# Decayed linear attention and two FFNs on one core: scores in tiles of 64 by 64, quarter-megabyte loads, one update moved ahead

## The chip, the core and the metric

The kernel runs on one core of a Trainium2 chip. Its engines work side by side: PE (TensorE) does the matmuls, DVE (VectorE), ACT (ScalarE) and POOL (GpSimd) work on tiles in the on-chip memory, and SP (SyncE) issues the DMAs, which 16 DMA engines carry out. Each engine runs its own instructions in order and waits on semaphores for the others. The metric is the device time of one execution in microseconds, lower is better, as a median over several runs.

## The reference

Per batch and head (2 by 8, sequence 768, head size 64), attention goes through blocks of 64 tokens and carries a 64 by 64 state:

```
intra = (q_b k_b^T * Dmask) v_b            Dmask[i,j] = lam^(i-j) for i >= j, else 0
inter = (q_b * lam^(pos+1)) state
out_b = intra + inter
state = lam^64 * state + (k_b * lam^(63-pos))^T v_b
```

The result, as 1536 tokens by 512, goes through two feed-forward layers with 2048 hidden units: h = x w_in; g = h * tanh(softplus(h)) in the first, g = h * relu6(h + 3) / 6 in the second; then g w_out.

## The kernel before, in words

Attention works on chunks of 128 tokens, two of the reference's blocks, all eight heads of a batch at once: 12 chunks, of which chunks 0 to 5 are one batch and 6 to 11 the other. A chunk's input `att[c]` is one row of 8 KB for each of 128 partitions, 1 MB: keys and queries with the head size down the partitions (columns 0 to 1023, two heads on the two halves of the partitions), then keys and values with the tokens down the partitions (columns 1024 to 2047). `load_raw(c, i)` loads half i of it, 512 KB.

What is done for a chunk, with the lines of the kernel before:

- `scores(c)` (line 194, PE): for each of 4 head pairs and each of its 2 heads, one matmul of a 64 by 128 weight tile (the keys) on 128 columns (the queries), into one of two PSUM banks by head. A float32 matmul leaves two records in the trace, so a chunk has 16.
- `weigh(c)` (line 216, DVE): the scores times the table of decays.
- `scale_k(c)` (line 206): the token-major keys times their decay, in place. For chunks 0 and 1 on DVE, else on POOL. `scale_q(c)` (line 210, POOL): the queries times theirs, once the scores have read them.
- `update(c)` (line 234, PE): scaled keys times values, weight tiles of 128 by 64, for the state that the next chunk needs.
- `attend(c)`: weighed scores times values (line 242, PE, weight tiles of 128 by 64), then state times scaled queries (line 248, PE, weight tiles of 64 by 64) unless the chunk starts a batch.
- `tokens(c)` splits the result into a high and a low part for the FFN (line 101 ACT, line 105 DVE), and `carry` inside it makes the next state (line 259 DVE; its fade on ACT or POOL).

The order on each engine is written out by hand: `hold` keeps program order on PE, DVE, ACT and POOL. After `warm_up(12)`, the tables, `scores(0)`, `warm_up(4)`, `scale_k(0)` and `weigh(0)`, the loop over c issues `update(c)`, for c = 0 also `scores(1)`, `weigh(1)` and `scale_k(1)` on DVE, then `attend(c)`, `scores(c + 2)`, `scale_q(c + 1)`, `tokens(c)`, `scale_k(c + 2)`, `weigh(c + 2)`. At chunks 8 to 10 the conversion of the first weight units is woven in (line 332 ACT, line 337 DVE).

All loads go through SP's queue in the order written (`follow`): the decay table, chunks 0 to 7, then after each of chunks 0 to 3 a chunk from 8 to 11, with the first two weight units (`load_w`, line 309, 512 KB each) between the halves of chunks 10 and 11, and three more weight units after them. The scheduler gives DMAs eight semaphores in turn, so that a DMA is issued once the one eight places before it has landed.

After the attention come the two FFNs, in 128-column tiles of the hidden units (lines 371 and 380, then 752 and 769), with weights converted from their packed form on the way.

Of the kernel before, what the change touches and what calls it, by code (L numbers as in the profile page):

```python
# [11 lines left out]
U16 = mybir.dt.uint16  # L12
# [10 lines left out]
def decay_attention__mish_ffn__hswish_ffn_kernel(  # L23
# [8 lines left out]
    nc = tc.nc  # L32
    NCH = att.shape[0]
# [8 lines left out]
    def hold(engine, ins):  # L42
        if engine in held:
            tc.keep_in_program_order(ins)
        return ins
# [38 lines left out]
    def two_banks(kind):  # L84
        i = bank_turn[kind]
        assert i % 2 == 0
        bank_turn[kind] = (i + 2) % len(BANKS[kind])
        return BANK[:, BANKS[kind][i]:BANKS[kind][i] + 2]
# [41 lines left out]
    def follow(ins):  # L130
        if loads:
            tc.add_manual_dep(
                ins.ins, loads[-1].ins.name,
                mybir.DependencyInfo(mybir.DependencyClass.NoSync, mybir.DependencyReason.DATA), reason="order of loads",
            )
        loads.append(ins)
    raw_t = {}
# [3 lines left out]
    def load_raw(c, i):  # L141
        if c >= NCH:
            return
        if i == 0:
            j = c % 8 - 4
            if j >= 0:
                raw_t[c] = early[:, 2048 * j:2048 * j + 2048]
            else:
                pool = lent_p if c % 4 > 1 else raw_p
                raw_t[c] = pool.tile([128, 2048], F32, tag="raw", name="raw")  # L150
        s = slice(i * 1024, (i + 1) * 1024)
        follow(nc.sync.dma_start(out=raw_t[c][:, s], in_=att[c, :, s]))  # L152

    def qk(c):
        t = raw_t[c]
        return (t[:, i:i + 512].rearrange("p (a i) -> p a i", a=4) for i in (512, 0))

    def kv(c):
        t = raw_t[c]
        return t[:, 1024:1536], t[:, 1536:2048]  # L160

    def reverse():
        rr = mask.rearrange("j h p i -> j p h i")[:, :, :, 127:128]
        return rr.to_broadcast([128, 4, 2, 64])

    def decay_tables():
# [9 lines left out]
        def powers(o, i, first, drive):  # L176
            tc.keep_in_program_order(nc.vector.tensor_tensor_scan(
                out=o, data0=small[:, i:i + 1].to_broadcast([128, 128]), data1=drive, initial=first,
                op0=ALU.mult, op1=ALU.add,
            ))  # L180
# [4 lines left out]
        for p in range(4):  # L185
            powers(lampow[:, p], p, 1.0, zero)

    def scores(c, kind):
        qT, kT = qk(c)
        sc = two_banks(kind).rearrange("p h (a i) -> p h a i", a=4)  # L190
        for p in range(4):
            for h2 in range(2):
                r = slice(h2 * 64, h2 * 64 + 64)
                hold("tensor", nc.tensor.matmul(sc[:, h2, p, :], lhsT=kT[r, p, :], rhs=qT[r, p, :], start=True, stop=True))  # L194
        sc_t[c] = sc

    def carries(c):
        return c % CPB < CPB - 1

    def follows(c):  # L200
        return c % CPB > 0

    def scale_k(c, name="gpsimd"):
        if carries(c):
            kk = kv(c)[0].rearrange("j (p h d) -> j p h d", p=4, h=2)
            hold(name, getattr(nc, name).tensor_tensor(out=kk, in0=kk, in1=reverse(), op=ALU.mult))

    def scale_q(c, name="gpsimd"):
        qT, kT = qk(c)
        hold(name, getattr(nc, name).tensor_tensor(out=qT, in0=qT, in1=lampow, op=ALU.mult))  # L210
# [3 lines left out]
    def weigh(c):  # L214
        out = masked[c] = amat[c % 2]
        hold("vector", nc.vector.tensor_tensor(out=out, in0=sc_t.pop(c), in1=mask, op=ALU.mult))  # L216

    half = [slice(0, 64), slice(64, 128)]

    def heads():  # L220
        for a in range(2):
# [5 lines left out]
    def update(c, kind):  # L227
        kn, vn = kv(c)
        uo = two_banks(kind)
        u = uo[:, 0, 256:512].rearrange("p (a d) -> p a d", a=4)  # L230
        uo_t[c] = u, uo[:, :, 0:256].rearrange("p b (a i) -> p b a i", a=2)
        if carries(c):
            for a, e, p, h2, s in heads():
                hold("tensor", nc.tensor.matmul(u[half[h2], p], lhsT=kn[:, s], rhs=vn[:, s], start=True, stop=True))  # L234

    def attend(c):
        qT, kT = qk(c)
        kn, vn = kv(c)
        o = [uo_t[c][1][:, i] for i in range(2)]
        last = not follows(c)  # L240
        for a, e, p, h2, s in sorted(heads(), key=lambda x: x[3]):
            hold("tensor", nc.tensor.matmul(  # L242
                o[h2][half[e], a], lhsT=vn[:, s], rhs=masked[c][:, h2, p, :],
                start=(a == 0), stop=(last and a == 1), skip_group_check=True,
            ))
        if follows(c):
            for a, e, p, h2, s in heads():
                hold("tensor", nc.tensor.matmul(  # L248
                    o[h2][half[e], a], lhsT=state[c % 2][half[h2], p, :], rhs=qT[half[h2], p, :],
                    start=False, stop=(a == 1), skip_group_check=True,  # L250
                ))
        del raw_t[c]
# [19 lines left out]
    def tokens(c):  # L272
        o = uo_t[c][1]
        off = (c % 4) * 128
        hi, lo = (X[c // 4][:, i, :, off:off + 128].rearrange("p (b a) i -> p b a i", b=2) for i in range(2))
        split_hi(hi, o)
        carry(c)
        split_lo(lo, hi, o)
# [2 lines left out]

    unit_turn = [0]
    SHARED = [(0, 1), (3, 0), (5, 0), (3, 1)]
    shared = {}
    busy = set()
    slots = {}

    def load_w(w, t, half, count):
        if w is w1 and count == 2:
            st = stage_p.tile([128, 2, 512], U64, tag="st2", name="st")  # L290
        elif w is w1 and (t, half) in SHARED:
            i, j = divmod(SHARED.index((t, half)), 2)
            if j == 0:
                shared[i] = stage_p.tile([128, 2, 512], U64, tag="st2", name="st")
            st = shared[i][:, j:j + 1]
        elif w is w1:
            i = unit_turn[0] % 3
            unit_turn[0] += 1
            slots[w is w1, t, half] = {i}
            st = ring[:, i:i + 1]  # L300
        else:
            i = unit[t // 2, half] % 2
            slots[w is w1, t, half] = {0, 1} if i == 0 else {3}
            st = ring[:, 0:2] if i == 0 else spare[0][:, 16:24].bitcast(U64).rearrange("p (t i) n -> p t (i n)", t=2)
        taken = slots.get((w is w1, t, half), set())
        assert not taken & busy
        busy.update(taken)
        words = w[t:t + count, half].rearrange("t p n -> p t n").bitcast(U16)
        ins = nc.sync.dma_start(out=st.bitcast(U16)[:, :, 0:2047], in_=words[:, :, 1:2048])
        if w is w1:  # L310
            follow(ins)
        stage_t[w is w1, t, half] = st

    def staged(w, t, half):
# [193 lines left out]
    def start_next(between=None):  # L508
        begin(*plan[begun[0]], between=between)
        begun[0] += 1  # L510
# [82 lines left out]
    warm_up(12)  # L593
    decay_tables()
    scores(0, "y")
    warm_up(4)
    scale_k(0, "vector")
    weigh(0)
    for c in range(NCH):
        update(c, "y" if c == NCH - 1 else "a" if c % 2 == 0 else "h")  # L600
        if c == 0:
            scores(1, "y")
            weigh(1)
            scale_k(1, "vector")
        attend(c)
        if c < NCH - 2:
            scores(c + 2, "y")
        if c < NCH - 1 and follows(c + 1):
            scale_q(c + 1)
        if c == 10:  # L610
            start_next(lambda: tokens(10))
        else:
            tokens(c)
        if c < NCH - 2:
            scale_k(c + 2)
        if c == 8:
            start_next(lambda: weigh(10))
        elif c < NCH - 2:
            weigh(c + 2)
        if c == 9:  # L620
            finish_next()
        if c < 4:
            load_raw(c + 8, 0)
            if c > 1:
                load_w(*plan[c - 2])
            load_raw(c + 8, 1)
        if c == 3:
            for i in (2, 3, 4):
                load_w(*plan[i])
# [12 lines left out]
    for n in range(STEPS):  # L642
# [23 lines left out]
        layer, k, t = seq[n][:3]  # L666
# [200 lines left out]
    for j in range(R):  # L867
        k, p = runs[j]
# [3 lines left out]
        for f, (name, ms) in enumerate(FILLS):  # L872
# [3 lines left out]
            c = COPY[name]  # L876
            hold("scalar", nc.scalar.activation(out=c, in_=bank_[:, 0:n], func=ACTF.Copy))  # L877
            c = c.rearrange("p (i n) -> p i n", n=256)
            if f == 1:
                hold("vector", nc.vector.tensor_tensor(  # L880
                    out=F[:, 2:4], in0=COPY["a"].unsqueeze(1).to_broadcast([128, 2, 256]), in1=c, op=ALU.add
                ))
            elif f == 2:
                hold("vector", nc.vector.tensor_tensor(
                    out=F[:, 0:4:3], in0=F[:, 3:4].to_broadcast([128, 2, 256]), in1=c, op=ALU.add
# [97 lines left out]
```

## Time and profile before

| | us |
|---|---|
| median of 3 runs (555.13 to 555.54) | 555.5 |
| the profiled execution's own time | 554.98 |
| its span | 553.2 |
| PE busy | 546.4 (99%) |
| DVE busy | 393.9 (71%) |
| ACT busy | 313.6 (57%) |
| POOL busy | 22.9 (4%) |

The span runs from the first to the last instruction that the profiler saw; the execution's own time has 1.8 us around it. A busy time is the sum of an engine's instructions, so 99% says that PE nearly always has something in it, not that it works at its peak. Weight loads (PEld) run beside the matmuls and are listed apart. In the rows "<-" in brackets is what ended the idle time ahead of an instruction.

### The profile page before, as it was taken

The numbers are of one execution on the slowest core, as the hardware profiler recorded it, in microseconds if no ns is written. First come the engines' busy times: TensorE is split into PE (matmuls) and PEld (weight loads), VectorE is DVE, ScalarE is ACT, GpSimd is POOL, SyncE is SP. The second block draws the span as 40 slices with busy tenths as digits, with TensorE's granted clock in tenths as the row PEclk, the third lists the DMA queues.
The fourth block names the chain that finished last, engine by engine and source line by source line (L and its number), as shares of the span: only waits on it lengthen the run. The fifth ranks groups of instructions, "written<-read, shape, count | busy, mean of one in ns | idle before, by whom it ended". The sixth has DMA issues, their size and how long they took to land.

```text
span 553.2 us, 9679 instructions
## 1 busy us (share of the span) xinstructions
PE 546.4 (99%) x3888; PEld 491.3 (89%) x3888; DVE 393.9 (71%) x613; ACT 313.6 (57%) x488; POOL 22.9 (4%) x24
## 2 busy tenths in 40 slices
PE   8999999999999999999999999999999999999997
PEld 4887888888888888888888999999999999999996
DVE  6668876551136757796772798887898887987776
ACT  2457898873255756867482555555455555454551
POOL 1761000000000000000000000000000000000000
PEclk9999999999999999999999999999999999999999
DMA  8995556450045998889979969994698975688912
GB/s 295 412 394 200 170 200 211 144 186 6 0 153 208 359 356 285 325 302 420 377 282 403 426 270 379 345 367 154 227 322 319 355 307 190 229 319 356 386 64 76
DMA packets 25356, 149.04 MB, mean 269 GB/s; under 512 B 2400, under 2 KB 5600, under 8 KB 18400
## 3 DMA queue, kind: packets, MB, share of 16 engines
q1 hardware_dynamic: 25312, 148.44, 70.6%
q8 instruction: 30, 0.49, 0.4%
q14 instruction: 14, 0.11, 0.1%
HBM read 115.92 MB, written 32.51 MB: 268 GB/s over the span
## 4 chain that ended last, share of the span: by engine, by line
PE 95%; DMA 2%; DVE 1%; ACT 1%; SPq 0%; issue 0%; DVEq 0%; ACTq 0%
PE bank L371 24%; PE bank L380 24%; PE bank L752 22%; PE bank L769 21%; PE bank L194 2%; DMA raw<-att 2%; PE bank L242 2%; PE bank L248 1%; PE bank L234 1%; SPq L152 0%; DVE FS L789 0%; DVE up L105 0%; DVE early L216 0%; ACT up L101 0%; DVE work L780 0%
## 5 line engine op out<-in xcount | busy, mean ns | idle before, releaser
L105 DVE TENSOR_TENSOR g<-x,g 128x512 fp32r<-128x512 f32 x48 | 33.0, 689 | 56.0 <-ACT g L401 52.4
L380 PE MATMUL bank<-g,up 128*128 128x512 f32 x288 | 70.3, 390 | 0.0
L371 PE MATMUL bank<-X,up 128*128 128x512 f32 x288 | 69.2, 389 | 0.0
L400 ACT ACTIVATE x<-bank 128x512 f32<-128x512 f32 x48 | 28.5, 593 | 70.7 <-PE bank L371 70.7
L371 PEld LDWEIGHTS bank<-X,up 128*128 128x128 f32 x288 | 54.1, 188 | 11.2
L380 PEld LDWEIGHTS bank<-g,up 128*128 128x128 f32 x288 | 53.6, 188 | 10.6
L877 ACT ACTIVATE two<-bank 128x512 f32<-128x512 f32 x48 | 28.7, 597 | 55.7 <-PE bank L752 55.7
L877 ACT ACTIVATE work<-bank 128x256 f32<-128x256 f32 (+1 forms) x48 | 23.6, 491 | 59.2 <-PE bank L752 59.2
L752 PE MATMUL bank<-X,up 128*128 128x256 f32 x384 | 54.6, 283 | 0.0
L752 PEld LDWEIGHTS bank<-X,up 128*128 128x128 f32 x384 | 49.9, 192 | 0.2 <-ACT work L877 0.2
L380 PE MATMUL bank<-g,lowA 128*128 128x512 f32 x180 | 43.2, 389 | 0.0
L371 PE MATMUL bank<-X,lowA 128*128 128x512 f32 x180 | 43.2, 389 | 0.0
L769 PE MATMUL bank<-up,lowB 128*128 128x256 f32 x318 | 43.1, 283 | 0.0
L780 DVE SCALAR_TENSOR_TENSOR work<-x,work 128x512 f32<-128x512 f32 x48 | 33.0, 688 | 14.0 <-ACT x L779 13.9
L769 PEld LDWEIGHTS bank<-up,lowB 128*128 128x128 f32 x318 | 40.3, 192 | 0.0
L371 PEld LDWEIGHTS bank<-X,lowA 128*128 128x128 f32 x180 | 33.8, 188 | 7.0
L380 PEld LDWEIGHTS bank<-g,lowA 128*128 128x128 f32 x180 | 33.8, 188 | 7.0
L107 DVE SCALAR_TENSOR_TENSOR lowA<-spare,lowA 128x1792 fp32r<-128x1792 f32 x16 | 32.4, 2022 | 10.3 <-ACT lowA L101 10.3
L752 PE MATMUL bank<-X,lowA 128*128 128x256 f32 x270 | 38.2, 283 | 0.0
L769 PE MATMUL bank<-up,up 128*128 128x256 f32 x276 | 37.7, 283 | 0.0
L752 PEld LDWEIGHTS bank<-X,lowA 128*128 128x128 f32 x270 | 35.2, 192 | 0.3
L769 PEld LDWEIGHTS bank<-up,up 128*128 128x128 f32 x276 | 35.1, 192 | 0.0
(122 smaller groups left out, 979.8 us busy)
## 6 DMA issues: line engine op xcount, KB each, us to landing
up<-wc SPq DMA_DIRECT2D x19, 1792.0 KB, 10.1
wc<-lowA SPq DMA_DIRECT2D x16, 1792.0 KB, 10.0
lowA<-wc SPq DMA_DIRECT2D x13, 1792.0 KB, 8.6
ring<-w SPq DMA_DIRECT2D x24, 511.8 KB, 3.5
raw<-att SPq DMA_DIRECT2D x16, 512.0 KB, 10.2
ring<-w SPq DMA_DIRECT2D x8, 1023.5 KB, 7.7
spare<-w SPq DMA_DIRECT2D x8, 1023.5 KB, 8.3
lowB<-wc SPq DMA_DIRECT2D x6, 1280.0 KB, 7.3
```

What stands on the lines that cost most here:

```text
L105: hold("vector", nc.vector.tensor_tensor(out=lo, in0=src, in1=f32(hi), op=ALU.subtract))
L107: hold("vector", nc.vector.scalar_tensor_tensor(out=lo, in0=src, scalar=scale, in1=f32(hi), op0=ALU.mult, op1=ALU.subtract))
L194: hold("tensor", nc.tensor.matmul(sc[:, h2, p, :], lhsT=kT[r, p, :], rhs=qT[r, p, :], start=True, stop=True))
L234: hold("tensor", nc.tensor.matmul(u[half[h2], p], lhsT=kn[:, s], rhs=vn[:, s], start=True, stop=True))
L242: hold("tensor", nc.tensor.matmul(o[h2][half[e], a], lhsT=vn[:, s], rhs=masked[c][:, h2, p, :], start=(a == 0), stop=(last and a == 1), sk ...
L371: hold("tensor", nc.tensor.matmul(h, lhsT=W[t][:, a, kt * 128:kt * 128 + 128], rhs=X[k][:, b, kt, :], start=(kt, a, b) == order[0], stop=( ...
L380: hold("tensor", nc.tensor.matmul(y[e], lhsT=l, rhs=r, start=(first and i == 0), stop=(last and i == 2),))
L400: hold("scalar", nc.scalar.activation(out=x, in_=h, func=ACTF.Mish))
L752: hold("tensor", nc.tensor.matmul(bank_[:, 256 * i:256 * i + 256], lhsT=w[:, a, kt * 128:kt * 128 + 128], rhs=x[:, b, kt], start=(i == 0 a ...
L769: hold("tensor", nc.tensor.matmul(acc[:, i], lhsT=GB[j % 2][:, gi, a, i * 128:i * 128 + 128], rhs=w[:, b], start=(first and i == 0 and q = ...
L780: hold("vector", nc.vector.scalar_tensor_tensor(out=F, in0=x, scalar=6.0, in1=F, op0=ALU.min, op1=ALU.mult))
L877: hold("scalar", nc.scalar.activation(out=c, in_=bank_[:, 0:n], func=ACTF.Copy))
```

## The change

Scores become 16 matmuls of 64 by 64 weight tiles in place of 8 of 64 by 128: the keys' 128 tokens are taken in two halves, which go to the two halves of the PSUM partitions. A raw half is loaded by two DMAs of 256 KB, and so are five weight units of the first layer; the number of DMAs in flight gets no rule of its own. Chunk 2's scores and weighing move from chunk 0's turn to chunk 1's, behind `update(1)`; chunk 1's `scale_k` moves from DVE to POOL.

```diff
--- before.py
+++ after.py
@@ -148,8 +148,9 @@
             else:
                 pool = lent_p if c % 4 > 1 else raw_p
                 raw_t[c] = pool.tile([128, 2048], F32, tag="raw", name="raw")
-        s = slice(i * 1024, (i + 1) * 1024)
-        follow(nc.sync.dma_start(out=raw_t[c][:, s], in_=att[c, :, s]))
+        for j in (2 * i, 2 * i + 1):
+            s = slice(j * 512, (j + 1) * 512)
+            follow(nc.sync.dma_start(out=raw_t[c][:, s], in_=att[c, :, s]))
 
     def qk(c):
         t = raw_t[c]
@@ -185,13 +186,16 @@
         for p in range(4):
             powers(lampow[:, p], p, 1.0, zero)
 
+    half = [slice(0, 64), slice(64, 128)]
+
     def scores(c, kind):
         qT, kT = qk(c)
         sc = two_banks(kind).rearrange("p h (a i) -> p h a i", a=4)
         for p in range(4):
-            for h2 in range(2):
-                r = slice(h2 * 64, h2 * 64 + 64)
-                hold("tensor", nc.tensor.matmul(sc[:, h2, p, :], lhsT=kT[r, p, :], rhs=qT[r, p, :], start=True, stop=True))
+            for m in half:
+                for h2 in range(2):
+                    r = half[h2]
+                    hold("tensor", nc.tensor.matmul(sc[m, h2, p, :], lhsT=kT[r, p, m], rhs=qT[r, p, :], start=True, stop=True))
         sc_t[c] = sc
 
     def carries(c):
@@ -214,8 +218,6 @@
     def weigh(c):
         out = masked[c] = amat[c % 2]
         hold("vector", nc.vector.tensor_tensor(out=out, in0=sc_t.pop(c), in1=mask, op=ALU.mult))
-
-    half = [slice(0, 64), slice(64, 128)]
 
     def heads():
         for a in range(2):
@@ -281,6 +283,7 @@
 
     unit_turn = [0]
     SHARED = [(0, 1), (3, 0), (5, 0), (3, 1)]
+    FIRST_UNITS = [(0, 0), (1, 0), (2, 0), (0, 1), (3, 0)]
     shared = {}
     busy = set()
     slots = {}
@@ -306,9 +309,11 @@
         assert not taken & busy
         busy.update(taken)
         words = w[t:t + count, half].rearrange("t p n -> p t n").bitcast(U16)
-        ins = nc.sync.dma_start(out=st.bitcast(U16)[:, :, 0:2047], in_=words[:, :, 1:2048])
-        if w is w1:
-            follow(ins)
+        ends = (0, 1024, 2047) if w is w1 and (t, half) in FIRST_UNITS else (0, 2047)
+        for a, b in zip(ends, ends[1:]):
+            ins = nc.sync.dma_start(out=st.bitcast(U16)[:, :, a:b], in_=words[:, :, a + 1:b + 1])
+            if w is w1:
+                follow(ins)
         stage_t[w is w1, t, half] = st
 
     def staged(w, t, half):
@@ -601,9 +606,12 @@
         if c == 0:
             scores(1, "y")
             weigh(1)
-            scale_k(1, "vector")
+            scale_k(1)
+        elif c == 1:
+            scores(2, "y")
+            weigh(2)
         attend(c)
-        if c < NCH - 2:
+        if 0 < c < NCH - 2:
             scores(c + 2, "y")
         if c < NCH - 1 and follows(c + 1):
             scale_q(c + 1)
@@ -615,7 +623,7 @@
             scale_k(c + 2)
         if c == 8:
             start_next(lambda: weigh(10))
-        elif c < NCH - 2:
+        elif 0 < c < NCH - 2:
             weigh(c + 2)
         if c == 9:
             finish_next()
```

## Rows read from the trace of the kernel before

**Rows 1.** the page, part 4: the chain that ended last, share by engine.

```profile
PE 95%; DMA 2%; DVE 1%; ACT 1%; SPq 0%; issue 0%; DVEq 0%; ACTq 0%
```

**Rows 2.** stretches: us, each engine's busy time (instructions), clock, DMA share, GB/s.

```profile
45.28:537.00 491.72, 491.72 (x3075) 446.61 (x3072) 351.57 (x545) 292.05 (x441) 0.00 (x0) 1.00 0.71 270
```

**Rows 3.** chain of waits, first 46 us: start us, us, what.

```profile
3.15 9.24 DMA raw<-att
12.44 1.16 PE bank L194 x16
```

**Rows 4.** PE's weight loads in time, 17.9 to 21.5 us: start, us, line, shapes.

```profile
18.20 0.43 PEld L248 LDWEIGHTS bank<-raw,state 64*64 64x64 f32 x16 [0.17 <-issue]
18.79 0.97 PEld L194 LDWEIGHTS bank<-early 64*128 64x128 f32 x16 [0.17 <-issue]
19.89 0.55 PEld L234 LDWEIGHTS bank<-raw 128*64 128x64 f32 x16
20.35 0.86 PEld L242 LDWEIGHTS bank<-early,raw 128*64 128x64 f32 x16
21.38 0.21 PEld L248 LDWEIGHTS bank<-raw,state 64*64 64x64 f32 x8 [0.17 <-POOL early L210]
```

**Rows 5.** the same, 8.3 to 10.2 us.

```profile
8.38 0.55 PEld L234 LDWEIGHTS bank<-raw 128*64 128x64 f32 x16 [0.42 <-DVE raw L206]
8.99 0.97 PEld L194 LDWEIGHTS bank<-raw 64*128 64x128 f32 x16
```

**Rows 6.** the same, 12.3 to 16.8 us.

```profile
13.53 0.55 PEld L234 LDWEIGHTS bank<-raw 128*64 128x64 f32 x16
13.99 0.86 PEld L242 LDWEIGHTS bank<-early,raw 128*64 128x64 f32 x16
```

**Rows 7.** POOL in time, 8 to 28 us: start, us, line, operation.

```profile
10.25 1.27 POOL L210 TENSOR_TENSOR raw<-raw,lampow 128x512 f32<-128x512 f32 x1 [9.81 <-PE bank L194]
13.77 1.06 POOL L206 TENSOR_TENSOR raw<-raw,mask 128x512 f32<-128x512 f32 x1 [2.25 <-DMA raw<-att]
```

**Rows 8.** SP's issue of chunk 11's first half; its KB and us to landing.

```profile
26.52 0.33 SPq L152 DMA_DIRECT2D raw<-att  x1
...
raw<-att SPq DMA_DIRECT2D x1, 512.0 KB, 10.5
```

**Rows 9.** landing of the decay table; issue to landing over line 152.

```profile
small<-lam SPq DMA_DIRECT2D x1, 70.0 KB, 2.1
...
DMA to landing us min/median/max: 4.9/10.2/11.4
```

**Rows 10.** DMA of 15:25, 340:344, 503:505.2 and 1.5:2.25 us; last number: share of 16 engines.

```profile
DMA packets 1120, 4.10 MB, mean 410 GB/s; under 512 B 124, under 2 KB 124, under 8 KB 1118
q1 hardware_dynamic: 1118, 4.07, 101.3%
...
DMA packets 140, 1.65 MB, mean 412 GB/s; under 512 B 15, under 2 KB 15, under 8 KB 15
q1 hardware_dynamic: 140, 1.65, 98.8%
...
DMA packets 338, 0.95 MB, mean 434 GB/s; under 512 B 48, under 2 KB 48, under 8 KB 304
q1 hardware_dynamic: 338, 0.95, 108.2%
...
DMA packets 121, 0.06 MB, mean 84 GB/s; under 512 B 9, under 2 KB 121, under 8 KB 121
q1 hardware_dynamic: 121, 0.06, 37.9%
```

**Rows 11.** PE's weight loads in time, 36 to 45.5 us.

```profile
40.05 0.97 PEld L194 LDWEIGHTS bank<-raw 64*128 64x128 f32 x16 [0.17 <-issue]
43.51 0.85 PEld L242 LDWEIGHTS bank<-early,raw 128*64 128x64 f32 x16 [0.44 <-DVE early L216]
```

**Rows 12.** ACT in time, 35 to 46 us.

```profile
37.51 0.65 ACT L332 ACTIVATE tops<-ring 128x512 f16<-128x512 bf16 x1
```

## The prediction, made before the changed kernel was run

> **What bounds the kernel now.** I read the page first: the chain that ended last is 95% TensorE [rows 1]. Then the stages: from 45.28 to 537 us PE is busy for 491.72 of 491.72 us, without a gap [rows 2]. All edits lie before that stretch (the first weight units feed it), so whatever brings its first matmul forward brings the end forward by as much, provided the weights keep up. The question is only: when does the stretch that begins at 45.28 us begin?
>
> For that I read the chain of waits of the first 46 us. It runs through the first loads until 12.39 us, when the first half of chunk 2 lands, and its scores start at 12.44 us [rows 3]; from there it is PE nearly throughout. So the attention has two limits in turn: landing until 12.4 us, then PE. I then took PE's weight loads in order of time, because their starts show when one group of matmuls gives way to the next. A middle chunk reads 18.20 (line 248, state times query), 18.79 (line 194, scores), 19.89 (line 234, updates), 20.35 (line 242), 21.38 (line 248 again): 3.18 us [rows 4].
>
> **Part 1: scores in 64 by 64 tiles.** Line 194 loads 64 by 128 tiles and takes 19.89 − 18.79 = 1.10 us for 16 records (8 float32 matmuls, two records each). The new form is 16 matmuls, 32 records, of the very form of line 248: a 64 by 64 weight tile, 128 columns moved, alternating over both row halves and both column halves. Line 248 takes 18.79 − 18.20 = 0.59 us for 16 records. What of that is the change of tile shape behind it? Line 234 takes 0.46 us where line 242, of its own weight shape, follows [rows 4], and 8.99 − 8.38 = 0.61 us where line 194 follows [rows 5]: a change costs 0.15 us. So line 248's form costs 0.44 us per 16 records, plus 0.15 us where the shape changes next. New scores: 2 × 0.44 + 0.15 = 1.03 us, only 0.07 us less than 1.10. The larger gain is at the neighbour: where scores follow line 248 directly, the change between them goes. Before: 0.59 + 1.10 = 1.69 us; after: 3 × 0.44 + 0.15 = 1.47 us; 0.22 us saved. Scores 3 to 7 and 9 to 11 follow a line 248: 8 × 0.22 = 1.76 us. Scores 8 follow line 242 (chunk 6 starts a sequence) and scores 2 will stand between lines 234 and 242: 2 × 0.07 = 0.14 us. Scores 0 and 1 lie before the landing that binds and count nothing. Bounds: no gain (1.10 us and both changes kept) to 1.90 us; a loss, 32 records at line 194's own 69 ns, is excluded by line 248's 37 ns. I take the full sum, since line 248 is the same form with operands of the same shape.
>
> **Part 2: chunk 1's update ahead of chunk 2's scores.** Before, PE idles until 12.44 us for chunk 2, then runs scores 2 to 13.53, update 1 to 13.99, and attend 1 [rows 6]. After, the 0.46 us of update 1 runs inside the idle time, if its scaled keys are there. They now come from POOL, which takes 1.06 us for such a scaling and had nothing before 10.25 us [rows 7]. Chunk 1's second half is the load ahead of chunk 2's first, so it lands near 11.1 at the 1.30 us per half of part 3, and its key quarter half a load earlier, 10.4; POOL is done near 11.6, update 1 near 12.1. Behind it on POOL waits the query scaling of chunk 1 (1.27 us, to about 12.9), needed by line 248 near 14.8. DVE loses one operation and gains none. Gain: 0.46 us; bounds 0 (keys late) and 0.46.
>
> **Part 3: loads in quarter megabytes.** Bytes and order stay; 24 raw loads become 48 and 5 weight loads 10. SP's issue takes 0.33 us, against about 0.65 us that a quarter megabyte takes to move, so SP keeps ahead. A half takes 10.5 us from issue to landing [rows 8], which is 8 halves at 1.30 us: about eight loads are outstanding. Eight new ones are 2 MB, some 5.3 us of data, still above the 2.1 us that the small first load takes and the 4.9 us of the first raw half [rows 9]; the queue should not run dry.
>
> What does change is the packet: 2 KB in place of 4 KB. From 15 to 25 us, 1118 − 124 = 994 packets of 4 KB took 101.3% of 160 us: 163 ns each. From 340 to 344 us, 125 packets of 13.2 KB took 63.2 us: 506 ns; the line through the two gives 86 ns at 2 KB. The one kind of stretch that holds 2 KB packets (503 to 505.2 us: 304 − 48 = 256 of them beside 34 of about 12.5 KB, 480 ns by that line) leaves (38.1 − 16.3) / 256 = 85 ns. Lower bound 81.5 ns, half of 163. Upper bound 92 ns, on the line to the 560-byte packets from 1.5 to 2.25 us (37.9% of 12 us over 112: 41 ns) [rows 10]. I take 85, the row that holds such packets. Two of them are 4.3% more than one of 163. Chunk 2's first half landed at 12.39 us and chunk 11's at 26.52 + 10.5 = 37.0 us, 19 halves later (two weight units among them): 1.30 us each [rows 3, 8]. So each half megabyte adds 0.056 us: chunk 2 (the 5th half) lands 0.28 us late, at 12.67; chunk 3 (the 7th) at 12.39 + 2 × 1.30 + 0.39 = 15.38; chunk 11 (the 24th) at 37.0 + 1.34 = 38.35.
>
> The Trainium skill, DMA: Bandwidth & Descriptors, Specifications, puts the least transfer for line rate at 512 B. By that rule 2 KB packets would cost nothing, and the sum would be that of the first rival below; the rows of this trace lean against it, as 4 KB in 163 ns is slower per byte than 13.2 KB in 506.
>
> **Walk through the attention.** Scores 2 start at 12.71 (12.67 and the 0.04 us seen between landing and start), line 242 of chunk 1 at 13.74 against 13.99, line 248 at 14.77; scores 3 could follow at 15.21 but wait until 15.42: 0.21 us. From there PE is the limit and gains 0.22 us a chunk. PE would reach scores 11 at about 38.25, but their queries land at 38.35: 0.15 us with the start. At the end, line 242 of chunk 11 had waited 0.44 us in the weight loads for DVE's weighing [rows 11]; that wait should go, but line 248 behind it then waits for the last state: 0.1 us net gained. The first weight unit is converted on ACT at 37.51 [rows 12]; it is two halves ahead of chunk 11's first, so it lands near 35.6, about when ACT now gets there, and the second near 39.7, likewise; ACT then has 2 us until its next piece of the state's chain. The later units are converted after 46 us, microseconds after they land.
>
> Sum: −1.76 − 0.14 − 0.46 − 0.1 + 0.28 + 0.21 + 0.15 = −1.8 us. The profiled execution took 554.98 us (553.2 of span and 1.8 around it), so it would be 553.2; the median of the three runs is 0.5 above it, 555.5, so I say **553.7 us**.
>
> **Rivals.**
> - *The small packets cost nothing.* Then the last three terms go: −2.4 us, 553.1. For it: the lower bound, 81.5 ns. Against: the 85 ns.
> - *The tiles save nothing*: shapes still drain between line 248 and the scores, or 32 records don't overlap as 16 do. PE keeps 3.18 us a chunk, and only the early 0.46 less 0.28 and less some wait for chunk 3 stays: 555.4, no change. For it: twice the instructions for the same products, each bank written in two partition halves. Against: line 248 does just that.
> - *The load stream becomes the bound* (slower). Place: scores 11. It decides once chunk 11's half lands past about 40.2 us, 3.2 us later than now, or 0.135 us per half: a 2 KB packet of 90 ns, or a queue that runs dry with 2 MB in it. At 92 ns a half takes 1.30 × 184 / 163 = 1.47 us, chunk 11 lands at 41.1, its scores start 1.05 us later than the 40.05 of before [rows 11], and 0.35 of that comes back in shorter scores and the wait for DVE: +0.7, 556.2. For it: the first half needed 4.9 us to land, close to the 5.3 us that 2 MB hold. Against: 410 GB/s held through the whole stretch of 4 KB packets [rows 10], with little between the packets to lose.
>
> **Numbers.** Forecast 0.58, free packets 0.14, no saving by tiles 0.18, load-bound 0.10. About 0.2% (1.1 us) is what a measurement can tell from no change. The forecast's own range is 553.1 to 554.6; in a seventh of it landing takes more than 0.7 us of the gain. Faster: 0.14 + 0.50 = 0.64. Same: 0.08 + 0.18 = 0.26. Slower: 0.10. The range reaches from 552.9 to 555.9: it holds the first three cases and stops short of the last.
>
> **What would show it.** Right: line 248 followed by scores without the 0.17 us gap in the weight loads, 1.47 us from line 248 to line 234; update 1 done before chunk 2's scores, and those near 12.7 us; raw loads near 393 GB/s; the first matmul of line 371 near 43.4 us. Wrong: 3.18 us a chunk; scores that wait for raw in several chunks; a gap in PE after that first matmul, where a weight unit is late.

## The result and the profile after

The changed kernel took 558.98 us (median of 6 runs, 558.36 to 560.18) against 555.39 us for the kernel before (6 runs): a ratio of 1.0071, 95% interval 1.0060 to 1.0082. It is slower by 3.6 us where the forecast said faster by 1.8; 558.98 lies above the range. The profiled execution took 558.71 us (before: 554.98), so the two traces show the same difference, and they are compared below. Ratios and intervals, here and below, leave out four single executions that took 670 us or more.

The FFN is as it was. In the rows of stretches below, the first is the part of the attention in which the loads stream, the second the FFN, which answers to [rows 2]; the third is the stream again, in the kernel before.

```profile
12.00:40.00 28.00, 24.10 (x613) 20.45 (x612) 16.91 (x23) 10.83 (x32) 16.76 (x15) 1.00 1.02 363
...
48.52:541.00 492.48, 492.48 (x3081) 447.26 (x3078) 351.95 (x545) 292.93 (x442) 0.00 (x0) 1.00 0.71 269
...
12.00:40.00 28.00, 27.57 (x544) 23.62 (x544) 19.32 (x28) 12.43 (x34) 18.01 (x17) 1.00 1.03 410
```

From its first matmul on PE is again busy without a gap. But that stretch begins at 48.52 us, where it had begun at 45.28: 3.24 of the 3.7 us are lost ahead of it. From there to the last matmul the two traces keep step within 0.03 us, and the remaining 0.47 us come after PE's last matmul. In the 28 us from 12 to 40 us PE is busy for only 24.10; in the kernel before it was busy for 27.57 of the same 28 us, at 410 GB/s in place of 363.

PE's weight loads around a middle chunk, in order of time, answer to [rows 4]:

```profile
18.17 0.43 PEld L250 LDWEIGHTS bank<-raw,state 64*64 64x64 f32 x16 [0.17 <-issue]
18.55 0.92 PEld L198 LDWEIGHTS bank<-early 64*64 64x64 f32 x32
19.64 0.55 PEld L236 LDWEIGHTS bank<-raw 128*64 128x64 f32 x16 [0.17 <-issue]
20.10 0.86 PEld L244 LDWEIGHTS bank<-early,raw 128*64 128x64 f32 x16
21.13 0.42 PEld L250 LDWEIGHTS bank<-raw,state 64*64 64x64 f32 x16 [0.17 <-issue]
```

Line 250 to line 236 takes 19.64 − 18.17 = 1.47 us, as worked out, the gap ahead of the scores is gone, and the chunk takes 2.96 us where it took 3.18. So in this chunk the tiles save just what part 1 said. The start answers to [rows 5, 6]:

```profile
11.43 0.55 PEld L236 LDWEIGHTS bank<-raw 128*64 128x64 f32 x16 [0.52 <-POOL raw L210]
12.29 0.89 PEld L198 LDWEIGHTS bank<-raw 64*64 64x64 f32 x32 [0.31 <-issue]
13.35 0.85 PEld L244 LDWEIGHTS bank<-early,raw 128*64 128x64 f32 x16 [0.17 <-issue]
...
15.62 0.89 PEld L198 LDWEIGHTS bank<-raw 64*64 64x64 f32 x32 [0.81 <-issue]
```

Update 1 stands ahead of scores 2, and line 244 of chunk 1 starts at 13.35 us, 0.6 earlier than before (part 2); then scores 3 wait for their data until 15.62 us (part 3 said 15.42). The loss is in what comes next. These are the PE groups, in order of time, ahead of which PE stood idle in mid group; the last bracket is the idle time and what ended it:

```profile
27.50 0.87 PE L244 MATMUL bank<-early 128*64 128x128 f32 x11 [1.39 <-issue]
...
33.33 0.62 PE L236 MATMUL bank<-early 128*64 128x64 f32 x13 [0.70 <-issue]
...
39.44 0.27 PE L250 MATMUL bank<-raw,state 64*64 64x128 f32 x1 [1.00 <-issue]
...
44.78 0.34 PE L236 MATMUL bank<-raw 128*64 128x64 f32 x4 [0.65 <-issue]
```

"issue" says that the engine waited for nothing the profile shows: no semaphore, no data. The stops fall inside a group of like matmuls (11 of 16 behind the first, one of 16 behind the third), where the order of the kernel has no wait at all. No such row stands in the kernel before.

Pitches from scores to scores close the account. Scores 3 start at 15.65 us here and at 15.62 before; from there to the FFN it takes 32.87 us against 29.66, +3.21. Five of the nine intervals have no stop: 14.43 against 15.29 us, a gain of 0.86. The four with a stop take 18.44 against 14.37: a loss of 4.07. The stops cost more than the 3.74 us of their brackets: a single matmul's record lasts 0.27 us (the row at 39.44), while 16 of them in a row take 0.67 (line 250 at 14.38 us), so that they overlap, and a bracket begins only where the last record before the stop ends.

### The profile page after: what moved, and what is told of

Same layout as the page of the kernel before. It is cut to its first block, busy times and chain, and to the rows that moved or that the text cites. A ratio compares the mean times of both kernels' runs of the same rounds, so it can differ in the third digit from the quotient of the medians.

```text
span 556.9 us, 10114 instructions
## 1 busy us (share of the span) xinstructions
PE 546.1 (98%) x4080; PEld 490.5 (88%) x4080; DVE 393.6 (71%) x612; ACT 314.2 (56%) x488; POOL 23.8 (4%) x25
## 4 chain that ended last, share of the span: by engine, by line
PE 94%; DMA 2%; DVE 1%; issue 1%; ACT 1%; SPq 0%; DVEq 0%; ACTq 0%
PE bank L376 23%; PE bank L385 23%; PE bank L760 22%; PE bank L777 21%; DMA raw<-att 2%; PE bank L244 2%; PE bank L198 1%; PE bank L250 1%; PE bank L236 1%; SPq L153 0%; DVE FS L797 0%; DVE up L105 0%; ACT up L101 0%; DVE work L788 0%; DVE work L897 0%
```

## The experiments

Times are medians beside runs of the kernel before on the same chip (555.29 to 555.45 us). My theory after the result: PE takes its instructions in blocks of some 256 records, each block comes by a DMA of its own, and while the load stream fills the DMA engines it comes only some 6 us after the one before. Rivals: the tiles cost PE's own time; or the slower load stream holds PE up.

**One part at a time.** `tiles_only`, the kernel before with only this:

```diff
-                hold("tensor", nc.tensor.matmul(sc[:, h2, p, :], lhsT=kT[r, p, :], ...))
+            for m in half:  # and r = half[h2] for each of the two heads
+                    hold("tensor", nc.tensor.matmul(sc[m, h2, p, :], lhsT=kT[r, p, m], ...))
```

> The kernel before with 64 by 64 scores alone; loads stay half megabytes, the order stays. Fetch theory (PE's instructions come in blocks of 256 over the DMA engines, and with 160 instead of 128 records a chunk PE reaches the end of a block about 4.8 us after its start, before the next one is there): PE stops for 0.7 to 1.7 us at records 960, 1216, 1472 and perhaps 704, 3 to 5 us in all, against 1.9 us saved by the tiles: 556.5 to 559. Load theory (2 KB packets make the raw loads late): loads are as before, so the tiles give their gain: 553.4 to 553.8, no stops inside a group of matmuls.

Measured: 558.7 us, ratio 1.0070 [1.0057, 1.0083]. The tiles alone bring the whole loss, at 410 GB/s. Its waits of PE (us in total, times, longest), then two of the restarts, and then the stretches from one stop's end to the end of the next, with PE's and PEld's records in brackets:

```profile
PE bank L243 <- issue: 1.5, 1, 1.5
PE bank L235 <- issue: 1.3, 1, 1.3
PE bank L197 <- issue: 1.2, 1, 1.2
...
PE bank L249 <- issue: 0.3, 1, 0.3
```
```profile
33.99 0.39 PE L235 MATMUL bank<-early 128*64 128x64 f32 x6 [1.25 <-issue]
...
40.30 0.92 PE L197 MATMUL bank<-raw 64*64 64x128 f32 x25 [1.21 <-issue]
```
```profile
27.65:33.97 6.32, 5.03 (x127) 4.20 (x126) 3.85 (x5) 2.26 (x6) 4.14 (x5) 1.00 1.03 409
33.98:40.29 6.31, 5.09 (x126) 4.34 (x127) 2.99 (x6) 2.98 (x8) 2.23 (x3) 1.00 1.03 409
```

Each stretch holds 253 matmuls and weight loads; with the semaphore instructions on PE's queue the trace has exactly 256 from stop to stop, and so it has in the changed kernel. The four stops stand at the four places that the expectation had named. 256 is a property of the instruction stream, not of the chunks (160 records each). The DMA view of the same time has the other half:

```profile
DMA packets 132, 0.49 MB, mean 410 GB/s; under 512 B 15, under 2 KB 15, under 8 KB 131
q1 hardware_dynamic: 131, 0.48, 99.7%
q8 instruction: 1, 0.02, 5.6%
...
DMA packets 430, 1.56 MB, mean 411 GB/s; under 512 B 48, under 2 KB 48, under 8 KB 430
q1 hardware_dynamic: 430, 1.56, 102.9%
```

From 31.5 to 32.7 us (first group) one 16 KB packet of the queue named "instruction" runs; PE stops at 32.74 and goes on at 33.99 us. From 33.99 to 37.8 us (second group) there is none; the next one runs from 37.88 to 38.95 us, PE stands from 39.09 to 40.30. So the packet starts 3.9 us after PE has entered a block, takes 1.1 us on its one engine among the load packets, and PE goes on some 1.4 us after it: 6.3 us in all (3.9 + 1.1 + 1.4, rounded). In the changed kernel the stretches between restarts are 5.8, 6.1 and 5.3 us (33.33 − 27.50 and so on).

`loads_only` is the kernel before with the quarter-megabyte loads and split weight units alone, `half_loads` the changed kernel with half-megabyte loads, `old_scores` the changed kernel with the old scores.

```diff
# loads_only: + for j in (2 * i, 2 * i + 1): s = slice(j * 512, (j + 1) * 512) ... ; FIRST_UNITS in two DMAs
# half_loads: changed kernel, - these lines, + s = slice(i * 1024, (i + 1) * 1024)
# old_scores: changed kernel, - for m in half, + sc[:, h2, p, :], lhsT=kT[r, p, :]
```

> The kernel before with quarter-megabyte loads alone; 128 records a chunk as before. Fetch theory: a block lasts 6.3 us, just enough; 555.2 to 556.5, stops of under 0.5 us in all. Load theory: raw lands 3 us later by chunk 11 and PE waits for it: 557.5 to 559.

Measured: 556.7 us, 1.0031 [1.0016, 1.0046], no stop labelled issue, 367 GB/s. PE waited for data 1.7 us in all at the start, and 1.0 us near the end behind DVE's work:

```profile
PE bank L195 <- DMA raw<-att: 1.7, 2, 1.5
PE bank L243 <- DVE lowB L107: 1.0, 1, 1.0
```

That is 0.2 us above the range of the fetch theory and 0.8 below that of the load theory.

> The changed kernel with half-megabyte loads; 64 by 64 scores and the new order stay. Fetch theory: the stops at records 960, 1216, 1472 and 1728 stay, 3 to 4.5 us: 556.5 to 558.5. Load theory: all of the loss was the loads, so 553 to 553.8. Mixed (small packets lengthen each fetch): stops get shorter, 554 to 556.

Measured: 559.22 us, 1.0077 [1.0062, 1.0091], at 409 GB/s, with stops of 1.5, 1.3, 1.2 and 0.3 us as in `tiles_only`. Of the four stops that the fetch theory expected three came, the last one didn't, and a short one came earlier; the time is 0.7 us above its range. Half-megabyte loads don't help the tiles.

> The changed kernel with the 64 by 128 scores of before; quarter loads and the new order stay. Fetch theory: the stops go, update 1 ahead of scores 2 gives 0.4 us: 554.8 to 555.6. Load theory: nothing is won back, 558 to 559.5.

Measured: 556.68 us, 1.0025 [1.0015, 1.0035], no stop labelled issue, 355 GB/s, PE waits for raw and early data (2.6 us in all, the longest ahead of scores 11):

```profile
41.73 1.16 PE L197 MATMUL bank<-raw 64*128 64x128 f32 x16 [1.04 <-DMA raw<-att]
```

Both theories missed this time: the stops went, as the fetch theory said, but the quarter loads then cost what it had left out. The stops go with the tiles and come with them; the loads cost about 1.3 us where they are the bound, and next to nothing on top of the stops (558.98 with both, 558.7 with the tiles alone, 559.22 with the tiles and the new order).

**Is it PE's own time?** `more_work` gives PE work in which few records take long:

```diff
# tiles_only, and in attend(c):
+        if 2 <= c < 10:
+            warm_up(2)
```

> Tiles alone (558.7 us), and ahead of the attention matmuls of chunks 2 to 9 two bfloat16 matmuls of 128x128 with 512 columns whose result nobody reads: 0.43 us of PE time and 4 PE records a chunk, 3.4 us and 32 records in all. Theory A (records bound it): the 3.4 us go into the stops; what is added is 32 records at 6.29/256 us = 0.8 us, so 559.2 to 559.8, with smaller stops labelled issue (4.3 us of them in the kernel with tiles alone, 1 to 2 left). Theory B (the tiles cost PE's own time or a pause that each group brings with it): the work is added in full, 562.1, and the stops stay at 4 us.

The bank that these matmuls write is also one of those in which a chunk's output stands, so part of the attention's result is changed. Measured: 559.59 us, 0.9 over `tiles_only`; the profiled run was the slowest of four (560.41, 2.2 over its counterpart). 16 matmuls and 4.8 us of PE time (eight groups of 0.6 us) were added, and 0.9 to 2.2 of it came out at the end. What remains of the stops:

```profile
16.14 0.43 PE L197 MATMUL bank<-raw 64*64 64x128 f32 x2 [0.41 <-issue]
...
35.03 0.69 PE L235 MATMUL bank<-early 128*64 128x64 f32 x16 [0.68 <-issue]
```

The stops shrank from 4.3 to 1.1 us, and the profiled run's account closes: 4.8 us of work, less 3.2 of stops, and 0.6 of new waits for DVE's line 105, which reads an output bank, make the 2.2. PE had room for that work because it was waiting for records, not for its array: theory B's 562.1 is excluded.

**Is it the load stream that makes the blocks slow?** `tiles_less` and its control `old_less` (the same on the kernel before) drop four chunks' loads:

```diff
+        if c >= 8:
+            raw_t[c] = kept[c - 8]
+            return
```

> Tiles alone, with the loads of chunks 8 to 11 left out (their attention is computed from the data of chunks 0 to 3, so four of the twelve chunks are not the reference's); the loads of the first FFN units follow in their place, and the stream ends some 10 us sooner. Theory A (blocks of 256 PE records are slow because the load stream fills the DMA engines): the stops in the stream stay (one or two of 1.2 to 1.5 us), those after it go, and from there a chunk takes 2.96 us; the first FFN matmul starts at 45.5 to 46.5 us instead of 48.55. Rival (PE's records come no faster than 41 per us whatever the loads do): the stops go on at each 256 records to 45 us, and the FFN starts at 48.5.

> The control: the kernel before with the same loads left out. PE is never out of data there after 12.4 us, so nothing changes: first FFN matmul at 45.2 to 45.4, 555.4 us. If part of what tiles_less gains comes from the absent loads themselves, it shows here.

Measured: `tiles_less` 556.15 us, 1.0018 [1.0008, 1.0027], 2.5 us under `tiles_only`, first FFN matmul at 46.09 us, as theory A said; `old_less` 555.41 us (0.9994 [0.9984, 1.0004]), no change, though its profiled run was the fastest of them (554.20 us, FFN at 44.47). That run's start was early: scores 2 began at 11.69 us, against 12.44 in the trace of before, and the same loads had landed by 11.45 us in `tiles_only`, so that a single trace's start can differ by up to 1 us and the medians decide. Stretches of one block each in `tiles_less`:

```profile
27.85:33.05 5.20, 5.03 (x127) 4.20 (x126) 2.75 (x4) 1.66 (x4) 2.76 (x3) 1.00 0.65 258
33.05:37.90 4.85, 4.83 (x126) 4.32 (x130) 3.38 (x5) 2.26 (x8) 3.11 (x3) 1.00 0.02 3
37.89:42.46 4.57, 4.57 (x137) 4.05 (x131) 3.10 (x6) 3.34 (x6) 3.31 (x3) 1.00 0.01 4
```

In the stream this kernel still stops for 1.5 us (up to 27.89) and for 0.2 us at 21.29; at 33.07, behind the last instruction packet that ran among the loads, the stop is 0.2 us. Once the stream is over, the same tiles use a block in 4.85 and 4.57 us with PE busy throughout. Its DMA from 33.07 to 34.25 us, then to 35.6:

```profile
DMA packets 0, 0.00 MB, mean 0 GB/s; under 512 B 0, under 2 KB 0, under 8 KB 0
...
DMA packets 1, 0.02 MB, mean 12 GB/s; under 512 B 0, under 2 KB 0, under 8 KB 0
q8 instruction: 1, 0.02, 5.8%
```

The instruction packet now starts 1.2 us after the block's start, not 3.9. The rival (41 records per us whatever the loads do) falls.

**Fewer loads in flight.** `flight4`, `flight3` and `flight2` are `tiles_only` with a limit, `flight4_old` is the kernel before with a limit of four:

```diff
+        if len(loads) >= 4:
+            tc.add_manual_dep(ins.ins, loads[-4].ins.name, ...)   # waits until that load has landed
```

> Tiles alone, and each load of the stream issued only when the load four before it has landed: at most four half megabytes in flight instead of eight. Theory A1 (a block of PE instructions waits behind the data already queued at the DMA engines): the blocks come sooner, about half of the 4.5 us of stops goes, 556 to 557, and the time from a block's entry to the next falls from 6.3 us to 5 to 5.7. Theory A2 (a block takes 6.3 us whatever is queued, because it shares the engines packet by packet or has a fixed delay): the stops stay, 558.5 to 559.5. If four half megabytes hold too little for the stream (theory Q of the quarter loads), PE waits for chunks instead: GB/s in 12:40 us at 340 to 370 and waits labelled DMA.

> As flight4 with at most three half megabytes in flight. A1: the stops go almost wholly (blocks in under 5 us), but the stream falls to about 1.5 MB in 5 us = 300 GB/s and PE waits for data: 558 to 562, with waits labelled DMA and not issue. A2: stops as with tiles alone and waits for data besides: over 560.

> As flight4 with at most two half megabytes in flight; for the fetch alone, the time being lost to data (some 1 MB in 4.5 us, 230 GB/s, 565 to 575). A1: no stop labelled issue at all. A2: stops remain wherever PE has used up 256 records within 6 us.

> The kernel before with at most four half megabytes in flight, that is the bytes that eight quarter loads hold, in 4 KB packets. Theory Q (2 MB in flight hold too little): 12:40 us moves 370 to 390 GB/s and the time is 0.5 to 1.5 us over before. Theory P (only the packet's size costs): 405 to 410 GB/s and 555.4.

Measured: 557.4 us (1.0038 [1.0024, 1.0052]), 564.74, 573.85, and 555.71 us (1.0010 [0.9997, 1.0024]). `flight4` in its profile keeps two stops:

```profile
32.05 0.39 PE L240 MATMUL bank<-early 128*64 128x64 f32 x6 [0.55 <-issue]
...
38.09 0.92 PE L202 MATMUL bank<-raw 64*64 64x128 f32 x25 [0.94 <-issue]
```

The median lies between A1 and A2, and A1's reason doesn't hold. With half as many loads queued the instruction packet starts 1.7, 4.1 and 3.7 us into the blocks entered at 20.5, 25.7 and 32.05 us, at 380, 318 and 414 GB/s: neither the loads in the queue nor the rate orders these. PE also stood 1.6 us for data, which uses up a block more slowly. So a stream that runs delays the blocks, but its depth is not shown to be the lever. `flight3` (289 GB/s) and `flight2` (235 GB/s) lose 9.5 and 10.1 us in waits for data and show no stop. That fits both A1 and a PE too slow to use up its blocks, so their stops decide nothing; in `flight2` the granted clock was also 0.50 (1.2 GHz) from 14 to 20 us, after PE had waited 2.9 us for data. Their instruction packets say more: from 12 to 40 us the DMA engines are busy 84% and 74% of the time (99% in `flight4`), and four packets in a row start 0.6 to 2.6 us into their blocks in `flight3`, 0.1 to 2.5 in `flight2`. Where the engines have time to spare, the packets come sooner; whether fewer loads in the queue or the lower rate does it, these runs cannot part.

**Where the stream's rate went.** `pair_loads` keeps the half megabyte and halves the packet:

```diff
+        to, of = (x.rearrange("p (b i n) -> p b i n", b=2, i=2)[:, :, i] for x in (raw_t[c], att[c]))
+        follow(nc.sync.dma_start(out=to, in_=of))
```

> The kernel before with a chunk's two loads still of half a megabyte, but each of two pieces of 2 KB a partition (the first q and the first of k's two halves of the tile, the second the others), so that only the packet size changes and 8 loads in flight still hold 4 MB. Theory P (small packets cost the stream): the quarter loads' 367 GB/s in 12:40 us comes back, 0.6 to 1.3 us slower, 556.0 to 556.7. Theory Q (eight quarter loads in flight hold too little and the queue runs dry): 400 GB/s or more, and 555.4 to 556.0; chunk 2's first scores wait for the chunk's second load, up to 0.7 us of it.

Measured: 558.28 us, 1.0054 [1.0034, 1.0074], but at 390 GB/s. DMA from 12 to 40 us here, then in `flight4_old`:

```profile
DMA packets 5307, 10.91 MB, mean 390 GB/s; under 512 B 331, under 2 KB 331, under 8 KB 5303
...
DMA packets 2651, 9.70 MB, mean 346 GB/s; under 512 B 298, under 2 KB 298, under 8 KB 2646
q1 hardware_dynamic: 2646, 9.62, 92.5%
```

The time is missed by both theories, and not by the rate: chunk 0 now needs both of its loads, scores 0 start at 8.81 us instead of 6.32, after PE has stood idle for 2.4 us, and the granted clock falls to 0.50 (1.2 GHz), where it was 1.00 in the kernel before:

```profile
10.00:13.00 3.00, 3.00 (x23) 1.37 (x20) 1.23 (x1) 0.00 (x0) 0.00 (x0) 0.50 1.05 404
```

The four warm-up matmuls behind scores 0 take 1.89 us instead of 1.04, update 0 takes 1.12 instead of 0.69. Scores 2 start 2.71 us late, the first FFN matmul 2.67: the whole loss is in the start, and behind it PE waits for no data. As to rate, 2 KB packets alone cost 410 − 390 = 20 GB/s, what the forecast had taken (393). The quarter loads lost 43 to 55. Four half megabytes in flight, the bytes of eight quarter loads, move 346 GB/s with 4 KB packets; that speaks for theory Q as the rest, though the rate lies below what it said and the time, 0.3 us over, below it too. It doesn't settle it: there the engines were busy 92.5%, while in `loads_only` their packets filled 102%.

**Part 2, and tiles out of the stream.** `order_only` is part 2 alone, `late_tiles` adds tiles in scores 10 and 11:

```diff
# order_only: the changed kernel's loop; loads and scores as before
# late_tiles: order_only, and
+            for m in half if c >= 10 else [slice(0, 128)]:
```

> The kernel before with part 2 alone: chunk 1's keys scaled on POOL, scores 2 after update 1, half-megabyte loads and the old scores. The forecast's part 2: update 1 goes ahead of the wait for chunk 2's data, 0.46 us saved, so 554.9. Theory A (PE's instruction blocks come no faster than one of 256 records in 6.3 us while the loads run): the early PE work also spends its records earlier, so the next blocks are awaited and most of the 0.46 us is given back: 555.2 to 555.5. The verdict is read from the start of the first FFN matmul too (45.28 us before): 44.8 by the forecast, 45.1 to 45.3 by theory A.

> As order_only, but scores 10 and 11 in tiles of 64 by 64 (64 PE records more, all after 36 us). By the forecast's part 1 two tiled scores save 2 x 0.22 = 0.44 us over order_only. Theory A: the block entered near 38.7 us is used up 64 records earlier, near 43.4 instead of 45; if the fetch is still at its 6.3 us there, 1.3 to 1.6 us is lost; since the att loads end near 37 us and a fetch with lighter transfers took some 4.4 us, the next block should be there in time: 0 to 0.44 us better than order_only. The rival (tiles are slow wherever they stand): slower than order_only by 2 x 0.35 us or more.

Measured: 555.5 us (0.9998 [0.9988, 1.0008]) and 555.2 us (0.9997 [0.9988, 1.0007]); the first FFN matmul at 45.68 and 45.70 us, against 45.28. Part 2 alone gains nothing. PE in `order_only`:

```profile
12.79 0.69 PE L234 MATMUL bank<-raw 128*64 128x64 f32 x16 [1.31 <-POOL raw L208]
13.41 1.16 PE L196 MATMUL bank<-raw 64*128 64x128 f32 x16
```

With half-megabyte loads chunk 1's keys land only with its whole second half, at 11.54 us; POOL scales them until 12.75, and scores 2, now behind update 1, start at 13.41 instead of 12.44 us. Neither the forecast's 44.8 nor theory A's account held: the wait is for POOL. In the changed kernel the quarter load brings the keys alone, and update 1 ran at 11.43. `late_tiles` shows a stop of 0.67 us at 38.82 us, before the loads are over, and behind scores 11 PE's weight loads wait for DVE (0.36 us) in any case: no gain that stands out of the noise, and not the loss of its rival.

None of the runs beats the kernel before.

## Why the prediction was wrong

- **What bounds the kernel.** Right for the FFN: it moved as a block, matmul for matmul within 0.03 us. Wrong for the attention: "from there PE is the limit" took PE's matmuls for its limit. PE has a second one, the supply of its records. In the kernel before a block of 256 (258 matmuls and weight loads in the rows below, ends included) lasts 6.25 us, about as long as one took in `tiles_only`. Its instruction packets ended 1.3 to 1.8 us before PE reached the blocks that they brought, and where kernels stopped, PE went on 1.2 to 1.6 us after its packet: the kernel before was already at that limit, with next to nothing to spare, and nothing was to be seen:

```profile
13.20:19.45 6.25, 6.25 (x130) 5.33 (x128) 3.38 (x4) 2.49 (x8) 5.18 (x5) 1.00 1.03 416
19.46:25.70 6.24, 6.24 (x130) 5.31 (x128) 4.31 (x6) 3.21 (x11) 4.03 (x4) 1.00 1.03 408
```

- **Part 1, the step that failed.** The price of the tiles was right to the hundredth (1.47 us, 2.96 a chunk) and the sum over eight chunks was wrong: the text counted 32 records in place of 16, priced their time on the array and never their number. Matmuls and weight loads went from 128 to 160 a chunk; at 5.3 to 6.3 us per 256, the stretches between restarts above, that is 160 / 256 × 5.3 = 3.3 to 3.9 us a chunk against 2.96 of work, so the forecast's gain was given back in stops, and about 3 us more. The rival "the tiles save nothing" named two reasons, drains and records that don't overlap, and neither was it; its "twice the instructions" pointed at the right thing, but as time on the array. None of the forecast's signs of being wrong came, since none of them looked for a stop inside a group.
- **Part 2.** In the changed kernel it did what was said, and scores 2 started at 12.32 us, sooner than 12.71. But scores 3 then waited for their data until 15.65 us, where the forecast had 15.42 and the kernel before 15.62, so nothing of the gain was left. The gain needs the quarter loads of part 3: `order_only` has none, and in `old_scores` scores 3 start at 15.12 us and scores 4 then wait 0.62 us for data.
- **Part 3.** A 2 KB packet costs about what was worked out (390 GB/s in `pair_loads`, forecast 393), but "the queue should not run dry" was too sure: 363 GB/s, not 393, and 1.3 us in `loads_only` against the 0.64 us of the three terms. In the changed kernel this came on top of nothing, since PE was late by its stops.
- **The rival on the slower side** put the wait at scores 11 for data. The end was slower, but scores 11 never waited for data in the changed kernel; the loss of 3.2 us has another place and mechanism. In `old_scores`, without the tiles, scores 11 did wait there for 1.04 us: the stops had hidden what this rival described.

The Trainium skill, Runtime: NRT & Kernel Launch, Instruction fetch mechanics, says that engines take instructions in blocks of 16 KiB, 256 instructions, by a DMA queue of their own, and that crossing a block's border is mostly hidden. The traces agree on the block (256 records, one 16 KB packet). On the hiding they agree for the kernel before and for `tiles_less` once its stream is over; in the changed kernel four crossings cost 0.65 to 1.39 us each.

The Trainium skill, DMA: Bandwidth & Descriptors, Specifications, puts the least transfer for line rate at 512 B, which would have given the time of the forecast's first rival. This is not borne out here: 2 KB packets moved 390 GB/s where 4 KB moved 410.

What stays open: how the 3 to 4 us until a packet's start come about while loads run, and why PE goes on only 1.2 to 1.6 us after its end; the last wait in `loads_only` (1.0 us, put down to DVE's line 107), whose reason I did not look for; and the split of the quarter loads' other 23 to 35 GB/s.

## What to carry to other kernels

Count an engine's instructions per microsecond as a resource beside its busy time: splitting matmuls into more of them can be free on the array and still stop the engine where large loads fill the DMA engines. A stop labelled "issue" inside a group of like instructions, at a fixed number of records, is the sign; the rows of the instruction queue in the DMA view date it. Before adding instructions to a stretch, compare the time that 256 of them will last with what the trace shows a block to take there.

## What was not expected of the hardware

- While loads ran at 409 GB/s, PE with the tiles alone got 256 records per 6.3 us, about 41 per us; without loads it used up a block in 4.57 us without a stop.
- With at most four half megabytes in flight instead of eight the kernel before ran at 346 GB/s instead of 410 from 12 to 40 us, and took 0.3 us longer, within what can be told apart: its stream has slack there.
- Of two kernels with 2 KB packets, the one with half-megabyte loads moved 390 GB/s and the one with quarter megabytes 367.
